# An opening list in another order, with statistics, inverse root and weight scale in smaller pieces and fewer dummy matmuls

## The chip, the core and the metric

The kernel runs on one core of a Trainium2 chip. The metric is the device time in microseconds (us) of one execution. The core has five engines that run side by side, each through its own instructions in order: TensorE (PE, matrix products), VectorE (DVE), ScalarE (ACT), GpSimd (POOL), and SyncE (SP), which here issues the DMA transfers. They wait for one another by semaphores. PE multiplies into PSUM banks, and what it has written there is read by DVE and ACT.

## What is computed

x has 2048 rows of 448 numbers. It is normalized row by row, goes through a filter in the frequency domain, and through an MLP with a gate; the results and x are added.

```python
def reference(A_x, A_w_r, A_w_i, B_x, B_W_gate, B_W_up, B_W_down):
    x = A_x
    xn = (x - mean) / sqrt(var + 1e-5)               # over the 448 columns
    A = irfft2(rfft2(xn) * (w_r + 1j * w_i))         # over rows and columns
    gate = xn @ W_gate                               # 448 x 1792
    up = xn @ W_up
    h = gate * (gate > 0) * up
    return x + A + h @ W_down                        # 1792 x 448
```

## The kernel before, in words

The rows are cut into 16 tiles of 128 (named by n2), and these into 4 chunks of 4 tiles; chunk q holds the tiles q, q+4, q+8 and q+12. The chunks come in the order 0, 2, 1, 3. The 1792 columns of W_gate and W_up are cut into 14 slabs f of 128, with g = 0 for gate and g = 1 for up. The slabs form groups of 5, 5 and 4; each group's part of h @ W_down is accumulated in PSUM for a chunk (dn, L923), with x or the sum so far as its start (dn_seed, L916, on ACT).

Products have nearly the precision of float32: each operand is split in two float16 parts, hi and lo, and three products are added (hi by hi, lo by hi, hi by lo). For weights, ACT writes hi (w_hi, L801) and DVE lo (w_lo, L805), after a common power of two has been found from the sum of the squares (w_sq, L189 on ACT; w_sum, L192 on POOL; w_scale, L195 and L199 on DVE). For a tile of rows the statistics (ln_stats, L255 and L258), the root (ln_sd, L266, ACT), the inverse root with one Newton step (ln_rstd, L271 to L276, DVE) give the normalized rows (ln_xn, L295); hi is made on ACT (L302, L304), lo on DVE (L332), and small rearranging copies on POOL (L311, L312, L333).

A matmul needs these tiles transposed, with the 448 columns on the partitions. The transposed tile of a chunk is named T; T_62 is that of the first chunk, T_63 that of the second. For the first chunk PE transposes against an identity matrix (L351), and the result is copied out of PSUM by DVE (vev, L359) or ACT (aev, L357); one block of 128 by 128 comes by a DMA transpose (d9, L345). From the second chunk on, the whole tile is transposed by DMA (dm, L341). A slab and chunk need 20 matmuls of 512 columns for each of gate and up (L852, gu; the first slab does them in halves of 256 columns), of which one step with only 64 partitions is shared by two slabs (L859). ACT then takes the positive part of the gate (L887), DVE multiplies it by up (L891), ACT writes its hi (L895) and DVE its lo (L899).

While all this runs, the Fourier part (L368 to L500 and L604 to L760) goes on beside it as background work, between the matmuls of the MLP.

Loads are issued by SP in order: x for statistics (load_xr, lx, L223, tiles y), x for the final sum (load_x, ly, L217, tiles xy), weight slabs (lw, L231, wst), W_down slabs (lwd, L241, wdst), Fourier constants (L245, fm), the identity (lid) and another constant, fd (lfd, both L1197).

**What sets the order.** The opening, up to the first group of 5 slabs of chunk 0, is written out by hand in OPENING (L29 to L41). Each word is a piece of work. In a block in which nothing is rescheduled (L1247 to L1257) the pieces are issued one after the other, so the list sets the order on every engine at once, DMA queue included. A piece is named by its step and its tile or slab: st0 is the statistics of tile 0, whiW0g1 the hi part of slab 0's up weights, tpA4 and tpB4 the first three and the other five transposes of tile 4, hh, lh and hl the three products of the first slab, gu2g1 all of slab 2's up, lo6 the lo part of tile 6, dm6 its DMA transpose. After the opening, a planner that counts the cost of each unit of PE work spreads the background work over the units; it starts from where the opening ended.

Dummy matmuls into spare PSUM banks (keep_warm, L1195, on a zeroed tile bw) stand at the beginning (warm, NWARM of them) and at three places in the opening (kw1, kw6, kw3).

## Time and profile before

| | |
| --- | --- |
| time, median of 3 runs | 443.38 us (443.28 to 443.58) |
| the profiled execution | 443.39 us |
| its span, first to last instruction | 441.6 us |
| mean granted TensorE clock | 0.999 |
| DMA, read from and written to HBM | 24.25 and 3.67 MB |

The span is what the engines' rows cover; 1.8 us of the time lie around it. In the rows below, a time is that from the start of the span, and of an engine's groups the count follows an x. "MATMUL gu<-T,wt" reads: the bank gu is written from T and wt. A bracket gives the idle time of the engine before the row, and which engine's tile ended it. SPq is SP's queue of transfers: its row says how long it took to issue, not how long the data took. A wait of an engine that waits for several things is put down to the one that came last.

### The profile page before, as it was taken

The numbers are of one execution on the slowest core, as the hardware profiler recorded it, in microseconds if no ns is written. First come the engines' busy times: TensorE is split into PE (matmuls) and PEld (weight loads), VectorE is DVE, ScalarE is ACT, GpSimd is POOL, SyncE is SP. The second block draws the span as 40 slices with busy tenths as digits, with TensorE's granted clock in tenths as the row PEclk, the third lists the DMA queues.
The fourth block names the chain that finished last, engine by engine and source line by source line (L and its number), as shares of the span: only waits on it lengthen the run. The fifth ranks groups of instructions, "written<-read, shape, count | busy, mean of one in ns | idle before, by whom it ended". The sixth has DMA issues, their size and how long they took to land.

```text
span 441.6 us, 8132 instructions
## 1 busy us (share of the span) xinstructions
PE 432.8 (98%) x3009; PEld 210.2 (48%) x3009; DVE 375.9 (85%) x922; ACT 254.3 (58%) x515; POOL 39.8 (9%) x84
## 2 busy tenths in 40 slices
...
GB/s 253 291 95 250 372 303 104 2 28 82 3 0 2 143 220 119 161 92 65 108 1 85 42 1 1 2 85 1 78 21 56 74 73 12 72 75 8 105 22 83
DMA packets 38360, 39.66 MB, mean 90 GB/s; under 512 B 18592, under 2 KB 33216, under 8 KB 38320
## 3 DMA queue, kind: packets, MB, share of 16 engines
...
q14 instruction: 17, 0.14, 0.1%
HBM read 24.25 MB, written 3.67 MB: 63 GB/s over the span
## 4 chain that ended last, share of the span: by engine, by line
PE 77%; DVE 13%; DMA 5%; SPq 2%; issue 1%; ACT 1%; POOL 0%; DVEq 0%; ACTq 0%
PE gu L852 44%; PE dn L923 23%; DMA sw<-wst 3%; PE gu L859 3%; PE fx L450 2%; DVE vt L715 1%; PE fx L417 1%; DVE g L891 1%; PE fx L723 1%; DMA y<-in_xr 1%; PE dn L955 1%; DVE h L899 1%; DMA xy<-in_x 1%; PE gu L955 1%; DVE wst L604 1%
## 5 line engine op out<-in xcount | busy, mean ns | idle before, releaser
L852 PE MATMUL gu<-T,wt 128*128 128x512 f16 (+1 forms) x1140 | 255.8, 376 | 1.6 <-DVE g L891 1.1
L852 PEld LDWEIGHTS <-wt 128*128 128x128 f16 x1140 | 108.7, 98 | 132.3 <-issue 10.7
L923 PE MATMUL dn<-wdt,h 128*128 128x448 f16 x624 | 127.6, 353 | 0.0
L923 PEld LDWEIGHTS <-h 128*128 128x128 f16 x624 | 60.2, 98 | 57.0
L895 ACT ACTIVATE h<-g 128x512 f16<-128x512 f32 x56 | 34.9, 626 | 65.1 <-DVE g L891 64.9
L887 ACT ACTIVATE g<-gu 128x512 f32<-128x512 f32 x56 | 33.0, 590 | 39.0 <-PE gu L859 23.5
L891 DVE SCALAR_TENSOR_TENSOR g<-gu,g 128x512 f32<-128x512 f32 x56 | 38.4, 686 | 18.6 <-ACT g L887 18.4
L899 DVE TENSOR_TENSOR h<-g,h 128x512 f16<-128x512 f32 x56 | 38.3, 685 | 6.0 <-ACT h L895 6.0
L927 ACT ACTIVATE xy<-dn,dsc 128x448 f32<-128x448 f32 x44 | 27.6, 630 | 25.1 <-PE dn L923 25.0
L192 POOL PARTITION_ALL_REDUCE wm<-wm x15 | 16.0, 1072 | 155.8 <-ACT junk L189 155.8
L916 ACT ACTIVATE dn<-xy,dinv 128x448 f32<-128x448 f32 x44 | 27.6, 632 | 0.5
L805 DVE SCALAR_TENSOR_TENSOR wt<-wst,wsc,wt 128x512 f16<-128x512 f32 x28 | 20.6, 748 | 1.0 <-ACT wt L801 1.0
L801 ACT ACTIVATE wt<-wst,wsc 128x512 f16<-128x512 f32 x28 | 19.2, 713 | 1.8 <-DVE wsc L199 1.8
L189 ACT ACTIVATE junk<-wst 128x512 bf16<-128x512 f32 x28 | 17.4, 621 | 0.9 <-DMA wst<-in_wgu 0.6
L859 PE MATMUL gu<-T,wt 64*128 64x512 f16 x112 | 17.0, 381 | 0.1
L732 DVE SCALAR_TENSOR_TENSOR wf<-fx,wf 128x512 f16<-128x512 f32 x16 | 10.9, 686 | 4.9 <-ACT wf L729 4.9
L255 DVE BATCH_NORM_STATS2 bst<-y 128x6 f32<-128x448 f32 x16 | 9.6, 613 | 5.8 <-DMA y<-in_xr 5.8
L440 ACT ACTIVATE Xh<-eo 128x464 f16<-128x464 f32 x16 | 8.9, 596 | 8.7 <-DVE eo L391 8.7
L710 ACT ACTIVATE vt<-wst,fsc 128x928 f16<-128x928 f32 x8 | 8.8, 1097 | 8.4 <-DVE wst L391 6.0
L470 DVE TENSOR_TENSOR y<-y,y 128x464 f32<-128x464 f32 x21 | 13.4, 638 | 0.2
L471 DVE TENSOR_TENSOR y<-y,y 128x464 f32<-128x464 f32 x21 | 13.4, 636 | 0.0
L723 PEld LDWEIGHTS <-vt 128*128 128x128 f16 x192 | 11.4, 98 | 2.0 <-issue 0.4
...
## 6 DMA issues: line engine op xcount, KB each, us to landing
...
```

Of the source, the lines that this page charges most:

```text
L189: A.activation(mt([128, 512], BF16, "junk")[:, 0:src.shape[-1]], src, AF.Square, scale=SQ, accum_out=acc)
L801: A.activation(w[:, 0:4, :], wst[f, g], AF.Copy, scale=wsc[f, g])
L805: V.scalar_tensor_tensor(w[:, 4:8, :], st, sc, w[:, 0:4, :], op0=OP.mult, op1=OP.subtract)
L852: last["P"] = P.matmul(hps[f, q][:, g, cs], wt[f, g][:, a, :], Tq[q][:, b, cs], start=(start and i == 0), stop=(stop and i == len(seq) - 1 ...
L859: m = P.matmul(hps[f, q][:, g, 0:512], wt[f, g][rows, 7, :], Tq[q][rows, b, :], start=start, stop=not start).ins
L887: last["A"] = A.activation(g1s[f, q], hps[f, q][:, 0, :], AF.Relu, scale=2.0 ** -22).ins
L891: last["V"] = V.scalar_tensor_tensor(g1, hps[f, q][:, 1, :], 2.0 ** -22, g1, op0=OP.mult, op1=OP.mult).ins
L895: A.activation(ht[f, q][:, 0, :], g1s[f, q], AF.Copy)
L899: V.tensor_tensor(h[:, 1, :], g1s.pop((f, q)), h[:, 0, :], op=OP.subtract)
L916: A.activation(dps[n2][:, 0:D], xy[n2], AF.Copy, scale=dinv[:, g:g + 1])
L923: last["P"] = P.matmul(dps[n2][:, 0:D], ht[f, q][:, a, js], wdt[f][:, b, :], start=False, stop=(f == fs[-1] and a == 1), skip_group_check= ...
L927: last["A"] = A.activation(xy[n2], dps[n2][:, 0:D], AF.Copy, scale=dsc[:, g:g + 1]).ins
```

## The change

1. NWARM goes from 19 to 14, and the three groups of dummies from 6, 3 and 1 to 5, 3 and 1, at other places.
2. OPENING is another order of nearly the same pieces. ln_stats becomes bn and ag, ln_rstd five pieces (ra to rm), w_scale wex and wsc, so that others may stand between them. Two evictions of the first tiles move from DVE to ACT (vevA0 and vevA4 become aevA0 and aevA4), one from ACT to DVE (aevB8 becomes vevB8).
3. Of the loads of x, ly0 and ly12 go from ahead of the DMA transposes to the end of the list, ly4 and ly8 stand ahead of them still. The DMA transposes of the ninth block (d9) come earlier in SP's queue, between weight loads, and lfd goes between two DMA transposes of the second chunk.
4. The tile bst gets 4 buffers for 2, and the hand list may begin a slab's bank with gate or up.

```diff
-NWARM = 19
+NWARM = 14
...
-lx0 lx4 lw lid lw lx8 lx12 lw lw lw lw lx2 lx10 lx6 lx14 lwd0 lwd1 lwd2 lwd3 lwd4 warm st0 st4 sqA rsA hi4
+lx0 lx4 bn0 bn4 ag0 ag4 sqA warm raA rbA rcA lw lid lx8 lx12 wsqW0g0 lw parW0g0 rdA rmA hi0 xn0 xn4 wexW0g0 lw cp0 lo0
...
-    def ln_stats(q, j):
-        n2 = q + 4 * j
-        st = ft([128, 6], F32, "bst", 2)
-        V.bn_stats(st, xr_t[n2])
+    def ln_bn(q, j):
+        bst[q, j] = ft([128, 6], F32, "bst", 4)
+        V.bn_stats(bst[q, j], xr_t[q + 4 * j])
+
+    def ln_ag(q, j):
         if j == 0:
             mv[q] = ft([128, 4, 2], F32, "mv", 2)
-        V.bn_aggr(mv[q][:, j, :], st)
+        V.bn_aggr(mv[q][:, j, :], bst.pop((q, j)))
...
-    def ln_rstd(q, js=(0, 1, 2, 3), bias=False):
+    def ln_r(step, q, js=(0, 1, 2, 3)):
...
+        if step == "a":
+            V.reciprocal(r0, sd)
+        elif step == "b":
...
+    def w_exp(f, gs=(0, 1)):
+        half_exponent(eg[:, f, gs[0]:gs[-1] + 1], state["wm", f][:, 1, gs[0]:gs[-1] + 1])
+
+    def w_pow(f, gs=(0, 1)):
         sc = mt([128, 2], F32, "wsc", 6)
-        e = eg[:, f, gs[0]:gs[-1] + 1]
-        half_exponent(e, state["wm", f][:, 1, gs[0]:gs[-1] + 1])
-        shift_exponent(sc[:, 0:len(gs)], e, -1, 188)
+        shift_exponent(sc[:, 0:len(gs)], eg[:, f, gs[0]:gs[-1] + 1], -1, 188)
...
-              **{f"kw{n}": (lambda n=n: keep_warm(n)) for n in (1, 3, 6)},
+              **{f"kw{n}": (lambda n=n: keep_warm(n)) for n in (1, 3, 5,)},
```

How the order moves is seen at three places. In the new order, lines of the program stand some 1 to 22 higher: L223 is L224, L266 is L274, L302 is L319, L357 is L374, L189 is L190, L801 is L823, L341 is L358, L891 is L913, L899 is L921, L443 is L460, L498 is L515, L859 is L881, and L1195 is L1217.

**ScalarE in the opening**, from the first root on. First the order before (tt_101 to tt_104 are the tiles of normalized rows, wt the weights' hi parts, junk,wm the sums of squares, fx the PSUM bank that PE transposes into):

```order
L266 ACTIVATE rs<-mv,eps 128x2
L302 ACTIVATE tt_101<-y_67,rs 128x448
L189 ACTIVATE junk,wm<-wst 128x512
L302 ACTIVATE tt_102<-y_66,rs 128x448
...
L801 ACTIVATE wt<-wst,wsc 128x512
...
L302 ACTIVATE tt_103<-y_68,rs 128x448
...
L302 ACTIVATE tt_104<-y_69,rs 128x448
...
L357 ACTIVATE T_62<-fx 128x3x128 x2
L357 ACTIVATE T_62<-fx 128x5x128 x2
```

And now:

```order
L190 ACTIVATE junk,wm<-wst 128x512
L319 ACTIVATE tt_101<-y_66,rs 128x448
L319 ACTIVATE tt_102<-y_67,rs 128x448
L374 ACTIVATE T_62<-fx 128x3x128
L823 ACTIVATE wt<-wst,wsc 128x512
L374 ACTIVATE T_62<-fx 128x3x128
L190 ACTIVATE junk,wm<-wst 128x512
L274 ACTIVATE rs<-mv,eps 128x2
L190 ACTIVATE junk,wm<-wst 128x512 x2
L319 ACTIVATE tt_103<-y_69,rs 128x448
L319 ACTIVATE tt_104<-y_68,rs 128x448
L374 ACTIVATE T_62<-fx 128x3x128 x2
```

A sum of squares has moved ahead of the first tile, and two evictions that DVE made before now stand among the first six rows. One eviction of five transposes follows behind, where before there were two.

**SP's queue from the second chunk's DMA transposes on**, before:

```order
L341 DMA_TRANSPOSE T_63<-tt_101 128x9x128
L341 DMA_TRANSPOSE T_63<-tt_103 128x9x128
L341 DMA_TRANSPOSE T_63<-tt_102 128x9x128
L341 DMA_TRANSPOSE T_63<-tt_104 128x9x128
L245 DMA fm<-in_c_fm 128x1024
L231 DMA wst<-in_wgu 128x512 x2
...
L217 DMA xy<-in_x 128x448 x4
L223 DMA y_82<-in_xr 128x448
L223 DMA y_83<-in_xr 128x448
```

And now (y_82 is the first tile of the third chunk, chunk 1):

```order
L358 DMA_TRANSPOSE T_63<-tt_103 128x9x128
L1219 DMA fd_t<-in_c_fd 128x464
L358 DMA_TRANSPOSE T_63<-tt_101 128x9x128
L358 DMA_TRANSPOSE T_63<-tt_104 128x9x128
L358 DMA_TRANSPOSE T_63<-tt_102 128x9x128
L246 DMA fm<-in_c_fm 128x1024
L232 DMA wst<-in_wgu 128x512 x2
L218 DMA xy<-in_x 128x448 x3
...
L218 DMA xy<-in_x 128x448 x2
...
L218 DMA xy<-in_x 128x448
L224 DMA y_82<-in_xr 128x448
L224 DMA y_83<-in_xr 128x448
```

The transposes come in another order of tiles, with fd's load behind the first. Between them and y_82 stood 10 loads (two fm, four wst, four xy); now there are 12, since six xy stand there. The rows left out repeat fm and wst.

**VectorE behind the statistics of chunk 1**, before:

```order
L330 SCALAR_TENSOR_TENSOR tt_104<-y_66,rs,tt_104 128x448
L330 SCALAR_TENSOR_TENSOR tt_104<-y_66,rs,tt_104 128x64
L891 SCALAR_TENSOR_TENSOR g_1038<-gu,g_1038 128x512
L498 TENSOR_TENSOR y_76<-y_77,fx 128x464
L499 TENSOR_TENSOR y_79<-y_77,fx 128x464
L443 TENSOR_TENSOR Xh<-eo,Xh 128x464 x2
L899 TENSOR_TENSOR h<-g_1038,h 128x512
```

And now:

```order
L347 SCALAR_TENSOR_TENSOR tt_104<-y_66,rs,tt_104 128x448
L347 SCALAR_TENSOR_TENSOR tt_104<-y_66,rs,tt_104 128x64
L515 TENSOR_TENSOR y_74<-y_73,fx 128x464
L516 TENSOR_TENSOR y_80<-y_73,fx 128x464
L460 TENSOR_TENSOR Xh<-eo,Xh 128x464 x2
L913 SCALAR_TENSOR_TENSOR g_1032<-gu,g_1032 128x512
L921 TENSOR_TENSOR h<-g_1032,h 128x512
```

The product of gate and up (L891, now L913), which frees two banks of PE, has moved behind four operations of the Fourier part. An L899 that stood behind the first statistics of chunk 1 now stands ahead of them.

More of the change, by code (lines that the diff above doesn't have):

```diff
@@ L279, in ln_rstd @@
         for i, j in enumerate(js):
-            rst[q, j] = r[:, i:i + 1], nm[:, i:i + 1], m[:, i, 0:1]
+            rst[q, j, "r"] = r[:, i:i + 1], nm[:, i:i + 1], m[:, i, 0:1]
+    def ln_rstd(q, js=(0, 1, 2, 3)):
+        for step in "abcdm":
+            ln_r(step, q, js)
     xn, tt, xn_b = {}, {}, {}
@@ L293, in ln_xn @@
         xn[n2] = xn_b[n2].rearrange("p g c k -> p (g c k)")[:, 0:D]
[L294 removed]
+        r, _, mean = rst[n2 % 4, n2 // 4, "r"]
         V.tensor_scalar(xn[n2], xr_t[n2], mean, r, op0=OP.subtract, op1=OP.mult)
@@ L1221, in gu_slab, with gu_part @@
     def gu_slab(f, g):
-        if f % 2 == 0 and g == 0:
+        if f % 2 == 0 and (f, q) not in hps:
             gu_open(f, q)
         gu_full(f, q, (g,), slice(0, 512), f % 2 == 0, f % 2 == 1)
+    def gu_part(f, q, *a):
+        if (f, q) not in hps:
+            gu_open(f, q)
+        gu_full(f, q, *a)
     for f in groups[0]:
```

61 lines of the change are left out of this document (35 added, 26 removed).

## The prediction

> **What bounds the kernel now.** I read the shares of the engines first, then the chain that ended last, then the list of what the TensorE (PE) waited for.
>
> ```profile
> PE 432.8 (98%) x3009; PEld 210.2 (48%) x3009; DVE 375.9 (85%) x922; ACT 254.3 (58%) x515; POOL 39.8 (9%) x84
> PE 77%; DVE 13%; DMA 5%; SPq 2%; issue 1%; ACT 1%; POOL 0%; DVEq 0%; ACTq 0%
> PE fx L351 <- DVE tt L332: 1.7, 2, 1.2
> PE dn L1195 <- POOL bw L1252: 1.5, 1, 1.5
> PE gu L852 <- DVE g L891: 1.1, 1, 1.1
> PE fx L351 <- ACT wt L801: 0.5, 1, 0.5
> ```
>
> PE is busy 98% of the span of 441.6 us, and its waits (total, times, longest) are few. Of those shown all but the 1.1 us for L891, late in the kernel, lie in the opening. So time can be won only in two ways: PE is given less to do, or its waits in the opening shrink. The opening matters beyond its waits, because it also holds dummy matmuls (L1195), which count as busy but compute nothing.
>
> ```profile
> 1.49 7.03 PE L1195 MATMUL dn<-bw 128*128 128x512 f16 x19 [1.49 <-POOL bw L1252]
> 10.62 1.46 PE L1195 MATMUL dn<-bw 128*128 128x512 f16 x6
> 12.80 0.81 PE L1195 MATMUL dn<-bw 128*128 128x512 f16 x3
> 15.54 0.44 PE L351 MATMUL fx<-id_t,tt 128*128 128x128 f16 x5
> 16.88 3.00 PE L852 MATMUL gu<-T,wt 128*128 128x256 f16 x26
> 19.90 0.60 PE L859 MATMUL gu<-T,wt 64*128 64x512 f16 x4
> 34.87 4.27 PE L852 MATMUL gu<-T,wt 128*128 128x512 f16 x19 [0.45 <-DVE wt L805]
> 39.07 0.61 PE L859 MATMUL gu<-T,wt 64*128 64x512 f16 x4
> 43.94 0.35 PE L923 MATMUL dn<-wdt,h 128*128 128x448 f16 x1
> 68.61 1.67 PE L852 MATMUL gu<-T,wt 128*128 128x512 f16 x7
> ...
> 1.40:7.00 5.60, 5.51 (x13) 1.00 0.80 241
> 7.00:8.30 1.30, 1.30 (x7) 1.00 0.96 351
> ```
>
> The first ten rows are PE's timeline (start, length, count, and in brackets the idle time before), the last two the windows of PE. Six dummies take 1.46 us and three 0.81 us, so one more costs (1.46 - 0.81) / 3 = 0.217 us at full pace. Up to 7.00 us 13 of them began, 5.60 / 13 = 0.43 us apart; behind it they are 0.22 apart (1.30 us for six intervals), although both rows give the granted clock as 1.00.
>
> **The change, part by part. Dummy matmuls.** 19 become 14, and groups of 6, 3 and 1 become 5, 3 and 1: six fewer. Fourteen at 0.43 from 1.49 end near 7.5, so the five that go are full-pace ones: 6 x 0.217 = 1.30 us less PE work. That becomes time only if what they covered is ready earlier. The next terms ask that.
>
> **First slab, set by ACT.** The changed order of ScalarE (ACT), shown with the change, has two more evictions of three transposes and one fewer of five.
>
> ```profile
> 6.29 0.76 ACT L302 ACTIVATE tt<-y,rs 128x448 f16<-128x448 f32 x1 [1.02 <-DVE rs L276]
> 8.22 0.62 ACT L189 ACTIVATE junk<-wst 128x512 bf16<-128x512 f32 x1
> 8.74 0.19 ACT L189 ACTIVATION_READ_ACCUMULATOR junk<-wst 128x1 f32 x1
> 9.80 0.29 ACT L266 ACTIVATE rs<-mv,eps 128x2 f32<-128x2 f32 x1 [0.87 <-DVE mv L258]
> 13.29 0.72 ACT L801 ACTIVATE wt<-wst,wsc 128x512 f16<-128x512 f32 x1 [0.61 <-DVE wsc L199]
> 15.30 0.49 ACT L357 ACTIVATE T<-fx 128x384 f16<-128x384 f16 x1
> ```
>
> The first normalized tile can end at 6.29 + 0.76 = 7.05 as before: the reordered statistics chain has the same steps, and the sum of squares now ahead of it in the queue fills ACT's 1.02 us of idle time. From there to the end of the last needed eviction ACT runs three more tiles (3 x 0.76), four evictions (4 x 0.49), two high halves of weights (2 x 0.72), three sums of squares (3 x 0.81) and one root (0.29): 8.40 us, hence 15.5 us. Behind it PE has 23 matmuls of 256 columns (3.00 / 26 = 0.115 each) and five transposes (at most 0.44): 3.0 us, so the first slab's last piece (L859) starts near 18.5, where it starts at 19.90 now. That is 1.4 us, about the 1.30 of the dummies; waits stay as long in sum as now. ACT idling would shrink it, and bounds are 0.5 and 2.5 us, but the next term caps the gain anyway. The split of statistics and inverse root adds no operation; VectorE (DVE) has three tensor copies where it had four. I cost the split at nothing: the small steps stand between larger ones of a queue that is full anyway, and if that cover went, each of them would cost PE some 0.2 us.
>
> **Transposes of the second chunk, the first cap.** PE reaches the second chunk's tile (T_63) at 39.07 with no wait. Freed of 1.4 us, and of the 0.45 us at 34.87 (that slab's VectorE half, L805, now stands three rows earlier in its order), PE would be there at 37.2. Then it meets SyncE's (SP's) transposes.
>
> ```profile
> 28.78 0.76 DVE L332 TENSOR_TENSOR tt<-y,tt 128x448 f16<-128x448 f32 x2
> 29.53 0.23 POOL L333 COPY tt<-tt 128x56 f16<-128x56 f16 x1 [7.91 <-DVE tt L332]
> 30.21 0.64 POOL L312 COPY tt<-tt 128x64 f16<-128x64 f16 x1
> 30.87 2.81 SPq L341 DMA_TRANSPOSE T<-tt  x2
> 34.29 2.74 SPq L341 DMA_TRANSPOSE T<-tt  x2
> 13.88 0.33 SPq L1197 DMA_DIRECT2D fd_t<-in_c_fd  x1
> ```
>
> Four transposes are queued at 1.4 us each, with 34.29 - 33.68 = 0.61 us of waiting for the third tile in between, and end at 37.03; PE's use at 39.07 bounds the landing at 2.04 us behind. In the new order the first of them is released by its own low half and its POOL copy. That low half has 71 VectorE operations ahead of it in either order, with one copy less and one small operation more now; before, the first transpose also stood behind two other tiles' POOL copies (29.53 to 30.85), now only behind its own. It can begin between 28.9 (PE's lead fully passed on, short copies) and 30.9 (nothing passed on); I take 29.7, PE's lead of 1.4 less what VectorE's full queue keeps. The load of fd now sits between the first and second transposes: +0.33. So 29.7 + 4 x 1.4 + 0.33 = 35.6 at the queue, and 37.7 landed. **PE gains 39.07 - 37.7 = 1.4 us here**, between 0.2 and 2.
>
> **Loads behind the transposes, the second cap.** Three things wait in SP's queue for the transposes: constants, weights, and rows of x for the residual (xy) and for chunk 1 (y). Two xy loads that stood ahead of the transposes now stand between them and y.
>
> ```profile
> 40.08 2.01 SPq L217 DMA_DIRECT2D xy<-in_x  x4
> 42.14 3.23 SPq L223 DMA_DIRECT2D y<-in_xr  x4
> 41.38 1.18 ACT L916 ACTIVATE dn<-xy,dinv 128x448 f32<-128x448 f32 x2
> 48.48 1.23 DVE L255 BATCH_NORM_STATS2 bst<-y 128x6 f32<-128x448 f32 x2 [2.21 <-DMA y<-in_xr]
> 52.49 0.64 DVE L368 TENSOR_TENSOR bw<-eo 128x464 f32<-128x464 f32 x1 [0.57 <-ACT eo L422]
> 57.87 1.19 DVE L443 TENSOR_TENSOR Xh<-eo,Xh 128x464 f16<-128x464 f32 x2 [0.60 <-ACT Xh L440]
> 66.63 0.68 DVE L891 SCALAR_TENSOR_TENSOR g<-gu,g 128x512 f32<-128x512 f32 x1
> 67.23 0.62 DVE L498 TENSOR_TENSOR y<-y,fx 128x464 f32<-128x464 f32 x1
> ...
> 40.00:50.00 10.00, 10.00 (x50) 4.59 (x47) 6.99 (x13) 5.43 (x11) 0.00 (x0) 1.00 1.00 369
> ```
>
> VectorE stands still 2.21 us for y until 48.48, the eleventh load behind the transposes; the last row (windows) shows all DMA engines busy then, 369 GB/s. In the new order y is the thirteenth: 448 KB more, 1.24 us at that rate. Counted from transposes that end 1.4 earlier, y lands at 48.48 - 1.4 + 1.24 = 48.3: as late by the clock as now, while PE is 1.4 ahead. VectorE then has, up to its next L891 (66.63, 18.15 us behind), three rows moved ahead of it and one taken out: two of L498's kind (0.62) and two of L443's (1.19 for both), less one of 0.66 (L899, estimated as L891): +1.8. Its two idle times of 0.57 and 0.60 go, since PE and ACT are ahead: -1.17. So that L891 ends at 48.3 + 18.15 + 1.8 - 1.17 + 0.68 = 67.8. PE wants its bank at 68.61 - 1.4 = 67.2. **Loss 0.55 us**, with bounds of 0 (no slow start of the loads) and 1.3 (the whole stretch from transposes to y grows in proportion, 11.4 us x 448 / 2656 KB = 1.9 in place of 1.24, which gives 1.2).
>
> The residual rows of the first accumulator now come fourth behind the transposes. By the same two rules they land between 40.0 and 42.6; ACT's seed (0.59 of the row at 41.38) has to follow before PE's first L923, at 43.94 - 1.4 = 42.5. Cost 0 to 0.7, **I take 0.15**.
>
> **Sum.** Against the profiled execution's own 443.39 us (span 441.6 and 1.8 around it; the median is 443.38): 443.39 - 1.4 + 0.55 + 0.15 = 442.7 us. Behind 70 us I expect a plain shift: PE's order reads alike in the last third, and its late wait of 1.1 us follows PE's own evictions.
>
> [...] The two windows above bear on the warm-up: pace 0.43, then 0.22, changing 5.5 us after the first dummy. [...]
>
> **The rivals.**
>
> (a) *No late stall.* y comes before 47.7, since the slow start of the queue is not repeated. For it: at 369 GB/s 2,656 KB need 7.4 us, and the stretch took 11.4. Then only the first cap holds: 443.39 - 1.4 = 442.0, or 441.7 with a faster start of the transposes. Chance 0.27.
>
> (b) *The change moves nothing measurable:* T_63 starts as late as now on VectorE's full queue, and fd's load in between eats the 0.3 left. The third tile's wait of 0.61 stays. Time 443.1 to 443.6. Chance 0.12.
>
> (c) *Slower: residual and y loads hold PE.* At the stretch's mean pace 13 loads take 13.3 us and y lands at 48.9; with a slow start that is 1 us longer it lands at 50, and L891 ends at 69.4 against 67.2: 2.2 lost, 1.4 won, and 0.3 lost on the seed: 444.5. It decides from a landing of 49.0 on, where gain and loss meet. VectorE is nearly full afterwards, so it cannot catch up:
>
> ```profile
> 80.00:100.00 20.00, 20.00 (x190) 9.90 (x189) 19.76 (x54) 15.03 (x29) 4.38 (x12) 1.00 0.12 23
> ```
>
> (third pair of numbers: VectorE 19.76 of 20 us). Against it: PE waited for nothing there before. Chance 0.10.
>
> (d) *Warm-up too short.* PE's pace is 0.43 until about 14 us. Then 9 dummies and about 17 matmuls of 256 columns each double (9 x 0.217 + 17 x 0.115 = 3.9), less 2.1 us of waits that they fill: +1.8, for 444.5. If it ends by 10.5, few matmuls are touched and the cost is about 0.2. Chance of the dear one 0.05.
>
> **How the numbers follow.** The forecast, 442.7 with its own range of 442.2 to 443.3, has 0.46; the rivals 0.27, 0.12, 0.10 and 0.05. A measurement of this kernel can tell about 0.2%, 0.9 us, from no change, so faster means below 442.5 and slower above 444.3. Faster: (a) and a quarter of the forecast, 0.39. Same: the rest of the forecast, (b) and some of (c), 0.47. Slower: 0.14. The range, 441.7 to 444.0, leaves out the dear ends of (c) and (d) and the low end of (a), some 0.2.
>
> **What would show it.** In the changed profile: L859's first group near 18.5; transposes into T_63 starting near 29.7 with fd's load between; PE's first T_63 matmul near 37.7 with some 0.5 us of wait ahead of it; VectorE's statistics on y at 48 to 48.6; a PE wait for L913 near 67. The prediction is wrong if statistics on y start before 47.5 (then (a)) or behind 49.0 (then (c)), if T_63 is used behind 38.7 (then (b)), if the dummies keep 0.43 behind 8.3 us (then (d)), or if PE shows waits between 70 and 300 us.

## The result, and the profile after

The changed kernel takes 447.92 us, median of 6 runs (446.83 to 449.6), against 443.48 (443.14 to 444.24) in as many of the kernel before: a ratio of 1.0101, with a 95% interval of 1.0074 to 1.0128. It is slower by some 4.5 us, and the forecast of 442.7 (441.7 to 444.0) was wrong, in sign and in size. The profiled execution took 449.6, its span is 447.8.

The engines' shares, the longest of PE's waits, and rows of PE's timeline in the changed kernel, which answer to the rows of before:

```profile
PE 435.4 (97%) x3003; PEld 210.3 (47%) x3003; DVE 374.8 (84%) x921; ACT 254.3 (57%) x516; POOL 43.4 (10%) x84
PE gu L881 <- DVE wt L827: 3.8, 1, 3.8
...
19.43 0.61 PE L881 MATMUL gu<-T,wt 64*128 64x512 f16 x4
32.62 1.03 PE L881 MATMUL gu<-T,wt 64*128 64x512 f16 x4 [3.85 <-DVE wt L827]
33.59 11.04 PE L874 MATMUL gu<-T,wt 128*128 128x512 f16 x40
44.56 0.60 PE L881 MATMUL gu<-T,wt 64*128 64x512 f16 x4
```

PE does six dummies less, yet it is busy for 2.6 us more (435.4 against 432.8). The first slab's last piece starts at 19.43, where it started at 19.90: 0.5 us won. Then stands a wait that the kernel before does not have, 3.85 us, ahead of the second pair of slabs. The 40 matmuls behind it take 11.04 us, where 40 took 8.81 before the wait. The second chunk's tile is reached at 44.56, where it was 39.07: 5.5 us behind. Of the 6.2 us by which the span is longer (447.8 against 441.6), these 5.5 stand there already.

Who holds PE? The wait is followed back through VectorE and ScalarE to SP's queue. These are the timelines of ScalarE, VectorE, SP (for SP: how long it took to issue) and POOL:

```profile
22.97 1.32 ACT L823 ACTIVATE wt<-wst,wsc 128x512 f16<-128x512 f32 x2
28.75 0.58 ACT L190 ACTIVATE junk<-wdst 128x448 bf16<-128x448 f32 x1 [4.46 <-DMA wdst<-in_wd]
30.60 0.57 ACT L909 ACTIVATE g<-gu 128x512 f32<-128x512 f32 x1
...
31.21 0.69 DVE L913 SCALAR_TENSOR_TENSOR g<-gu,g 128x512 f32<-128x512 f32 x1 [4.36 <-ACT g L909]
31.82 0.74 DVE L827 SCALAR_TENSOR_TENSOR wt<-wst,wsc,wt 128x512 f16<-128x512 f32 x1
...
12.28 5.25 SPq L362 DMA_TRANSPOSE T<-tt  x2
17.64 0.52 SPq L232 DMA_DIRECT2D wst<-in_wgu  x1
18.69 2.91 SPq L362 DMA_TRANSPOSE T<-tt  x1
23.21 1.38 SPq L242 DMA_DIRECT2D wdst<-in_wd  x3
...
16.18 0.39 POOL L350 COPY tt<-tt 128x56 f16<-128x56 f16 x2
```

Read it from PE backwards. PE waits until 32.62 for a low half of weights (L827), which VectorE begins at 31.82. VectorE is in order, and ahead of this stands a product of gate and up (L913, at 31.21) that waits 4.36 us for ScalarE's gate (L909, at 30.60). ScalarE is in order too: ahead of the gate stands the sum of squares of W_down's slab 0 (L190 on wdst), and for that load ScalarE stands still for 4.46 us, until 28.75. The load is the second of the three issued from 23.21 on, so it was issued near 23.7, and 5.1 us passed until ScalarE could use it. SP came to it so late because two small DMA transposes, put ahead of it, held SP from 12.28 to 17.53 (the second had to wait for its tile, whose last copies on POOL are the row at 16.18), and a third took 2.91 us to issue. In the kernel before, the five loads of W_down stood ahead of the transposes and of the weight loads that follow; this is its row:

```profile
9.46 3.01 SPq L241 DMA_DIRECT2D wdst<-in_wd  x5
```

Last, the clock. Windows of PE in the changed kernel (stretch, its length, busy time, then granted clock, DMA share and rate):

```profile
28.00:30.00 2.00, 0.77 (x4) 1.00 0.14 44
30.00:32.00 2.00, 0.00 (x0) 0.83 0.01 4
36.00:38.00 2.00, 2.00 (x6) 0.50 0.66 126
38.00:40.00 2.00, 2.00 (x11) 0.96 1.02 201
```

The granted clock falls to 0.50 inside the wait and comes back at about 38.2 (0.96 over the window from 38 to 40). PE starts 6 matmuls in the window at 0.50 and 11 in that at 0.96. That is why the 40 matmuls take 11.04 us, and not 8.81.

### The profile page after: what moved, and what is told of

Same layout as the page of the kernel before. It is cut to its first block, busy times and chain, and to the rows that moved or that the text cites. A ratio compares the mean times of both kernels' runs of the same rounds, so it can differ in the third digit from the quotient of the medians.

```text
span 447.8 us, 8119 instructions
## 1 busy us (share of the span) xinstructions
PE 435.4 (97%) x3003; PEld 210.3 (47%) x3003; DVE 374.8 (84%) x921; ACT 254.3 (57%) x516; POOL 43.4 (10%) x84
## 3 DMA queue, kind: packets, MB, share of 16 engines
q1 hardware_dynamic: 38320, 39.14, 28.8%
## 4 chain that ended last, share of the span: by engine, by line
PE 68%; DVE 13%; DMA 10%; SPq 4%; ACT 2%; issue 1%; POOL 1%; DVEq 0%; ACTq 0%
PE gu L874 39%; PE dn L945 20%; DMA sw<-wst 3%; PE gu L881 3%; DMA wst<-in_wgu 2%; PE fx L467 2%; DVE vt L732 1%; DMA fm<-in_c_fm 1%; PE fx L740 1%; DMA wdst<-in_wd 1%; DVE h L921 1%; DMA xy<-in_x 1%; PE dn L977 1%; DVE g L913 1%; DMA y<-in_xr 1%
## 5 line engine op out<-in xcount | busy, mean ns | idle before, releaser
L874 PE MATMUL gu<-T,wt 128*128 128x512 f16 (+1 forms) x1140 | 258.4, 378 | 2.6 <-DVE g L913 1.3
L913 DVE SCALAR_TENSOR_TENSOR g<-gu,g 128x512 f32<-128x512 f32 x56 | 38.3, 685 | 24.3 <-ACT g L909 24.1
L909 ACT ACTIVATE g<-gu 128x512 f32<-128x512 f32 x56 | 33.0, 589 | 43.6 <-PE gu L881 24.9
L921 DVE TENSOR_TENSOR h<-g,h 128x512 f16<-128x512 f32 x56 | 38.3, 685 | 9.3 <-ACT h L917 9.3
L827 DVE SCALAR_TENSOR_TENSOR wt<-wst,wsc,wt 128x512 f16<-128x512 f32 x28 | 20.5, 744 | 4.3 <-ACT wt L823 4.3
L881 PE MATMUL gu<-T,wt 64*128 64x512 f16 x112 | 17.4, 390 | 4.0 <-DVE wt L827 3.8
L823 ACT ACTIVATE wt<-wst,wsc 128x512 f16<-128x512 f32 x28 | 19.1, 713 | 0.1
L190 ACT ACTIVATE junk<-wst 128x512 bf16<-128x512 f32 x28 | 17.5, 624 | 2.7 <-DMA wst<-in_wgu 2.4
L328 POOL COPY tt<-tt 128x56 f16<-128x56 f16 x16 | 8.1, 508 | 54.2 <-ACT tt L337 51.3
```

What stands on the lines that cost most here:

```text
L190: A.activation(mt([128, 512], BF16, "junk")[:, 0:src.shape[-1]], src, AF.Square, scale=SQ, accum_out=acc)
L823: A.activation(w[:, 0:4, :], wst[f, g], AF.Copy, scale=wsc[f, g])
L827: V.scalar_tensor_tensor(w[:, 4:8, :], st, sc, w[:, 0:4, :], op0=OP.mult, op1=OP.subtract)
L874: last["P"] = P.matmul(hps[f, q][:, g, cs], wt[f, g][:, a, :], Tq[q][:, b, cs], start=(start and i == 0), stop=(stop and i == len(seq) - 1 ...
L881: m = P.matmul(hps[f, q][:, g, 0:512], wt[f, g][rows, 7, :], Tq[q][rows, b, :], start=start, stop=not start).ins
L909: last["A"] = A.activation(g1s[f, q], hps[f, q][:, 0, :], AF.Relu, scale=2.0 ** -22).ins
```

## The experiments

Theory T: the late load of W_down holds ScalarE's queue, and through it VectorE and PE. Rival C: the shortened warm-up lets the clock fall. Rival S: transposes among the loads slow all of them. For the smaller terms of the prediction further runs follow. Times are medians, the ratios against runs of the kernel before that were made with them on the same chip.

### Two loads exchanged

```diff
-bn10 wscW2 lh10 hl01 bn2 ag2 ag14 ag6 hl11 lwd4 wsqW3g1 parW3 lh11 hp0 gu1g1 re0 wexW3 whiW2g1 d90 ag10 wscW3 lwd2 lw
-whiW2g0 gu1g0 ly8 tm0 sqC raC whiW3g0 wloW2g1 lwd1 whiW3g1 lwd0 gu2g1 wdq0 rbC wsqW4g0 wloW3g0 rcC gh0 re1 lwd3
+bn10 wscW2 lh10 hl01 bn2 ag2 ag14 ag6 hl11 lwd0 wsqW3g1 parW3 lh11 hp0 gu1g1 re0 wexW3 whiW2g1 d90 ag10 wscW3 lwd2 lw
+whiW2g0 gu1g0 ly8 tm0 sqC raC whiW3g0 wloW2g1 lwd1 whiW3g1 lwd4 gu2g1 wdq0 rbC wsqW4g0 wloW3g0 rcC gh0 re1 lwd3
```

> The changed kernel with two words of the opening list exchanged: the load of W_down's slab 0 now stands where that of slab 4 stood, four loads earlier, and slab 4's in its place. Every instruction stays where it is on every engine. Theory T (the late load): in the changed kernel ScalarE stands still 4.46 us at 24.29 for W_down's slab 0, which lands at 28.67; behind it in ScalarE's queue is the gate of slab 1, behind that VectorE's low half of slab 3, and for this PE waits 3.85 us at 28.77. Now slab 0 should land near 23.6, ScalarE should not wait there, PE's 3.85 us should fall to under 1, the clock should stay at 1.00, and the time should be 442.5 to 444. [...] Rival S (the transposes among the loads slow every load): the wait only moves to slab 4's low-priority sum of squares, and 446 or more stays.

444.39 us, ratio 1.0019 (1.0009 to 1.0028), some 0.4 us above the expected range. 3.5 of the 4.5 us are gone with the exchange of two loads, and not one instruction of a compute engine has moved. PE's rows, then VectorE's row for y and SP's rows for the large transposes:

```profile
28.58 0.61 PE L881 MATMUL gu<-T,wt 64*128 64x512 f16 x4
39.09 0.61 PE L881 MATMUL gu<-T,wt 64*128 64x512 f16 x4 [0.77 <-DMA T<-tt]
69.56 4.48 PE L874 MATMUL gu<-T,wt 128*128 128x512 f16 x20 [0.61 <-DVE g L913]
...
49.92 1.24 DVE L257 BATCH_NORM_STATS2 bst<-y 128x6 f32<-128x448 f32 x2 [2.72 <-DMA y<-in_xr]
...
30.38 1.34 SPq L358 DMA_TRANSPOSE T<-tt  x1
32.45 4.46 SPq L358 DMA_TRANSPOSE T<-tt  x3
```

The wait at 28.8 is gone, and the clock stays at 0.999 or 1.000 in all ten runs. What is left are the waits that the prediction spoke of: the large transposes (0.77 at 39.09) and VectorE behind y (0.61 at 69.56). Rival C, for which the exchange of two loads changes nothing, and rival S fall as the cause of the large loss.

### The small transposes behind the loads

```diff
-wloW0g1 hh11 vevB8 aevB12 whiW1g0 wloW1g0 whiW1g1 d94 d912 wsqW2g1 wloW1g1 wsqW2g0 parW2 bn6 wsqW3g0 bn14 lw wexW2
-bn10 wscW2 lh10 hl01 bn2 ag2 ag14 ag6 hl11 lwd4 wsqW3g1 parW3 lh11 hp0 gu1g1 re0 wexW3 whiW2g1 d90 ag10 wscW3 lwd2 lw
-whiW2g0 gu1g0 ly8 tm0 sqC raC whiW3g0 wloW2g1 lwd1 whiW3g1 lwd0 gu2g1 wdq0 rbC wsqW4g0 wloW3g0 rcC gh0 re1 lwd3
-wloW2g0 rdC xn14 hi14 xn6 wsqW4g1 hi6 parW4 xn10 hi10 tm1 wloW3g1 cp10 cp14 xn2 gu2g0 wexW4 d98 wdq4 wdq2 lo10 dm10
+wloW0g1 hh11 vevB8 aevB12 whiW1g0 wloW1g0 whiW1g1 wsqW2g1 wloW1g1 wsqW2g0 parW2 bn6 wsqW3g0 bn14 lw wexW2
+bn10 wscW2 lh10 hl01 bn2 ag2 ag14 ag6 hl11 lwd4 wsqW3g1 parW3 lh11 hp0 gu1g1 re0 wexW3 whiW2g1 ag10 wscW3 lwd2 lw
+whiW2g0 gu1g0 ly8 tm0 sqC raC whiW3g0 wloW2g1 lwd1 whiW3g1 lwd0 gu2g1 wdq0 rbC wsqW4g0 wloW3g0 rcC gh0 re1 lwd3 d94 d90 d912 d98
+wloW2g0 rdC xn14 hi14 xn6 wsqW4g1 hi6 parW4 xn10 hi10 tm1 wloW3g1 cp10 cp14 xn2 gu2g0 wexW4 wdq4 wdq2 lo10 dm10
```

> The changed kernel with the four small DMA transposes (ninth block) put behind all W_down loads in SyncE's queue, as they stand in the kernel before; nothing else moves. Theory T, with the transposes as the cause that the loads are late: all five W_down loads land before 22 us, PE's wait of 3.85 us goes, 442.5 to 444. If the position of the W_down loads alone made them late, and the transposes among them cost nothing, W_down's slab 0 still lands behind 26 us and 446 or more stays. Rival C: no change, 447 to 450.

444.88 us, ratio 1.0033 (1.0020 to 1.0046). ScalarE's wait for the load shrinks from 4.46 to 0.74 us. Rows of SP and ScalarE:

```profile
9.86 6.17 SPq L232 DMA_DIRECT2D wst<-in_wgu  x3
17.97 1.38 SPq L242 DMA_DIRECT2D wdst<-in_wd  x3
24.68 0.58 ACT L190 ACTIVATE junk<-wdst 128x448 bf16<-128x448 f32 x1 [0.74 <-DMA wdst<-in_wd]
```

Slab 0's load, the second of the three, is issued near 18.45 here, 5.2 us earlier than in the changed kernel. So the transposes ahead of the loads cost these 5.2 us, and most of ScalarE's wait. They are not all of the lateness: in the kernel before, slab 0's load was issued at 9.46, and here SP stands until 15.7 in front of the third weight load, for a buffer that VectorE (L827, whose row there ends at 15.62) has to free. The expectation that all five loads land before 22 us was missed: ScalarE could use slab 0 only at 24.68, 6.2 us after its issue. The time came 0.9 us above the expected range; the large transposes started at 31.45 here, 1.1 us later than in the run before.

### Nineteen dummies at the beginning

```diff
-NWARM = 14
+NWARM = 19
```

> The changed kernel with 19 dummy matmuls at the beginning in place of 14; nothing else moves. Theory T: the wait of 3.85 us is set by a load and not by PE's pace, so it only shrinks by what PE arrives later (about 1 us), and the time stays at 446.8 to 449.6. Rival C (too short a warm-up): the clock stays at 1.00 and the time falls to 443 to 445.

447.94 us, ratio 1.0102 (1.0087 to 1.0117): as slow as the changed kernel, as T says and against rival C, which had 443 to 445. Rows of ScalarE and PE, and a window of PE:

```profile
26.97 0.58 ACT L190 ACTIVATE junk<-wdst 128x448 bf16<-128x448 f32 x1 [3.27 <-DMA wdst<-in_wd]
30.83 0.61 PE L881 MATMUL gu<-T,wt 64*128 64x512 f16 x4 [2.66 <-DVE wt L827]
...
32.00:34.00 2.00, 2.00 (x7) 0.56 0.00 0
```

ScalarE's 3.27 and PE's 2.66 differ by 0.61; in the changed kernel 4.46 and 3.85 differ by 0.61 too. The wait passes through one for one. It is shorter than in the changed kernel because slab 0 came 1.8 us earlier (26.97 against 28.75), and not because PE came later, as expected: PE stood from 28.17 on, where it was 28.77. The clock fell here too, near 32.2, 1.4 us behind the end of the wait.

### ScalarE's sum of squares moved, the loads left

```diff
-whiW2g0 gu1g0 ly8 tm0 sqC raC whiW3g0 wloW2g1 lwd1 whiW3g1 lwd0 gu2g1 wdq0 rbC wsqW4g0 wloW3g0 rcC gh0 re1 lwd3
-wloW2g0 rdC xn14 hi14 xn6 wsqW4g1 hi6 parW4 xn10 hi10 tm1 wloW3g1 cp10 cp14 xn2 gu2g0 wexW4 d98 wdq4 wdq2 lo10 dm10
+whiW2g0 gu1g0 ly8 tm0 sqC raC whiW3g0 wloW2g1 lwd1 whiW3g1 lwd0 gu2g1 rbC wsqW4g0 wloW3g0 rcC gh0 re1 lwd3
+wloW2g0 rdC xn14 hi14 xn6 wsqW4g1 hi6 parW4 xn10 hi10 tm1 wloW3g1 cp10 cp14 xn2 gu2g0 wexW4 d98 wdq0 wdq4 wdq2 lo10 dm10
```

> The changed kernel with its loads untouched, but the sum of squares of W_down's slab 0 moved back in ScalarE's own queue, behind the last tile of chunk 2, next to those of the slabs 4 and 2 (the order behind the opening changes by 68 of PE's rows with it). Theory T in its second half, that it is ScalarE's in-order queue that carries the late load to PE: ScalarE does not wait at 24.3, PE's wait at 28.8 is under 1 us, and the time is 443.5 to 445. If PE waited for a late weight load itself and not for the queue: 446.5 or more stays.

444.63 us, ratio 1.0022 (1.0013 to 1.0031). Slab 0's load is issued near 22.6, about as late as in the changed kernel (23.7 and, in its second profile below, 22.2), but PE does not wait at 28.6:

```profile
28.62 0.60 PE L881 MATMUL gu<-T,wt 64*128 64x512 f16 x4
```

The order behind the opening changed with this edit in some of PE's rows, but not ahead of this one. This shows the second half of T: the order of ScalarE's queue carried the load's delay to PE.

### The same in the kernel before

```diff
-lx0 lx4 lw lid lw lx8 lx12 lw lw lw lw lx2 lx10 lx6 lx14 lwd0 lwd1 lwd2 lwd3 lwd4 warm st0 st4 sqA rsA hi4
+lx0 lx4 lw lid lw lx8 lx12 lw lw lw lw lx2 lx10 lx6 lx14 warm st0 st4 sqA rsA hi4
...
-wloW0g1 lw lfd hh01 hh11 whiW1g0 st2 lh01 lh10 whiW1g1 hl01 wloW1g0 lw hl11 wsqW2g0 wloW1g1 lw ly0 ly4 ly8
+wloW0g1 lw lfd hh01 hh11 whiW1g0 st2 lh01 lh10 whiW1g1 hl01 wloW1g0 lw hl11 wsqW2g0 wloW1g1 lw lwd0 lwd1 lwd2 lwd3 lwd4 ly0 ly4 ly8
```

> The kernel before, with its five W_down loads moved in SyncE's queue from ahead of the last four weight loads to behind them, just ahead of the x rows and the small transposes; every instruction of the other engines stays in its place. Theory T (a late W_down load holds ScalarE's queue and through it PE): slab 0 of W_down then lands near 23, ScalarE, which wants it at 21.15, stands still for about 2 us there, PE gets a wait of 0.5 to 2 us near 28 that the kernel before does not have, and the time is 444 to 445.5. If the loss in the changed kernel came from something else of the new order, this stays at 443.0 to 443.8.

445.29 us, ratio 1.0041 (1.0028 to 1.0055). ScalarE's and PE's rows:

```profile
23.66 0.58 ACT L189 ACTIVATE junk<-wdst 128x448 bf16<-128x448 f32 x1 [2.58 <-DMA wdst<-in_wd]
26.65 4.48 PE L852 MATMUL gu<-T,wt 128*128 128x512 f16 x20 [1.77 <-DVE g L891]
```

Late loads of W_down alone, with no transposes ahead of them, make the kernel before slower by the same road: 2.58 us on ScalarE, 1.77 us on PE (here through VectorE's product L891).

### The wait filled with dummies

```diff
-cp6 wscW4 whiW4g0 hi2 wdq3 lfd hp2 gu3g1 gu3g0 lo6 re2 lo14 gl0 cp2 dm14 lo2 wdq1 tm2 wloW4g0 gh2 wdp whiW4g1 wdsc dm2
+cp6 wscW4 whiW4g0 hi2 wdq3 lfd kw17 hp2 gu3g1 gu3g0 lo6 re2 lo14 gl0 cp2 dm14 lo2 wdq1 tm2 wloW4g0 gh2 wdp whiW4g1 wdsc dm2
...
-              **{f"kw{n}": (lambda n=n: keep_warm(n)) for n in (1, 3, 5,)},
+              **{f"kw{n}": (lambda n=n: keep_warm(n)) for n in (1, 3, 5, 17)},
```

> The changed kernel with 17 dummy matmuls (17 x 0.216 = 3.7 us) just ahead of the PE instruction that waits 3.85 us, so that PE is busy through nearly all of the wait. It measures what the clock's drop behind the wait costs by itself (11.04 us for 40 matmuls in place of 8.81 in the profiled execution). If the drop follows from PE standing idle: no run shows a clock below 0.999, and the time is 446.5 to 447.2 in all of them, the level of the changed kernel's runs with clock 1.00. If it has another cause: some runs still come out near 449 with a clock of 0.992 to 0.996.

448.65 us (448.05 to 452.04), ratio 1.0117 (1.0100 to 1.0134). Four of five runs had a clock of 0.999 or 1.000, but at 448.05 to 449.33 they were slower than expected. In the fifth, the profiled one (0.996), it fell in a later wait. Its rows of PE and ScalarE, with 17 dummies up to the end of the first wait:

```profile
50.28 4.68 PE L945 MATMUL dn<-wdt,h 128*128 128x448 f16 x15 [2.20 <-ACT dn L938]
...
49.59 1.19 ACT L938 ACTIVATE dn<-xy,dinv 128x448 f32<-128x448 f32 x2 [5.25 <-DMA xy<-in_x]
```

So the filling kept the clock up at the first wait (1.00 in all windows from 28 to 42), but the times that were expected of that did not come. In the profiled execution PE lost 2.20 us to the residual rows, for which ScalarE stood still 5.25 us. The order behind the opening also differed in some of PE's rows, so what the clock costs is not measured by this run.

### The changed kernel once more

> The changed kernel once more, unedited, for the clock alone: of its six runs three had a mean granted clock of 0.992 to 0.996 and took 448.8 to 449.6, three had 0.999 to 1.000 and took 446.8 to 447.1. If a fall of the clock behind PE's wait of 3.85 us costs time by itself, the runs divide in the same two groups, some 2 us apart. If the division was chance (in the run with 19 dummies at the beginning it was not seen: 447.7 to 448.1 with the low clock, 448.4 with the full one), clock and time do not go together.

446.90 us, 445.51 to 449.87 in six runs, ratio 1.0093 (1.0068 to 1.0119). The one run with a low clock, 0.992, took 449.87, but one with 0.999 took 448.36, so the groups are not clean. Its profiled execution (446.42) shows why they spread; rows of SP, ScalarE and PE:

```profile
18.11 1.11 SPq L362 DMA_TRANSPOSE T<-tt  x1
25.86 0.58 ACT L190 ACTIVATE junk<-wdst 128x448 bf16<-128x448 f32 x1 [2.15 <-DMA wdst<-in_wd]
29.72 0.61 PE L881 MATMUL gu<-T,wt 64*128 64x512 f16 x4 [1.53 <-DVE wt L827]
41.19 0.61 PE L881 MATMUL gu<-T,wt 64*128 64x512 f16 x4 [0.77 <-DMA T<-tt]
```

Here the third small transpose took 1.11 us to issue, not 2.91, ScalarE waited 2.15 us, not 4.46, and PE 1.53, not 3.85; the clock stayed at 1.00 in all windows from 28 to 42. The same program has a wait of 1.5 to 3.9 us. Of the 2.9 us by which slab 0 came earlier here (25.86 against 28.75), 1.5 are its earlier issue (near 22.2 against 23.7), and 1.4 a shorter way from issue to use (3.7 us against 5.1). The transpose is thus only part of it: in the run with 19 dummies at the beginning it took 1.18 us, and the load still took 5.1 us. What sets that time is not shown. From the end of PE's wait to the second chunk's tile it took 41.19 - 29.72 = 11.47 us with the full clock, and 44.56 - 32.62 = 11.94 with the fallen one. The fall of the clock thus cost some 0.47 us in that execution, not the 2.2 us by which the matmuls were longer, since with the full clock PE waits 0.77 us for the transposes instead, and 0.89 at two places in between. In the run with 19 dummies at the beginning the clock fell as well, and the same way took 42.30 - 30.83 = 11.47 us, no longer than with the full clock.

### Six dummies less, in the kernel before

```diff
-NWARM = 19
+NWARM = 14
...
-xn4 xn0 wsqW0g0 cp4 st8 hi0 parW0g0 st12 wsqW0g1 cp0 tpA0 lo0 tpA4 kw1 wscW0g0 sqB tpB0 kw6 parW0g1 wsqW1g0
+xn4 xn0 wsqW0g0 cp4 st8 hi0 parW0g0 st12 wsqW0g1 cp0 tpA0 lo0 tpA4 kw1 wscW0g0 sqB tpB0 kw5 parW0g1 wsqW1g0
...
-              **{f"kw{n}": (lambda n=n: keep_warm(n)) for n in (1, 3, 6)},
+              **{f"kw{n}": (lambda n=n: keep_warm(n)) for n in (1, 3, 5)},
```

> The kernel before with the changed kernel's number of dummy matmuls (14 at the beginning, the group of six cut to five), nothing else moved. Theory T: the opening is set by the engines that feed PE, so six dummies less are worth little: PE starts the first slab at most 0.3 us earlier, and the time is 443.0 to 443.6, the same. If the dummies set PE's pace through the opening, as the prediction's first term has it: 442.1 to 442.4. If the warm-up becomes too short for the clock: 444 or more, with the granted clock or the dummies' spacing showing it.

443.92 us, ratio 1.0010 (0.9999 to 1.0020): no gain, as T expected, though 0.3 us above its range, and a hint of rival C. Five of eleven runs had a clock of 0.991 to 0.996 and took 443.9 to 444.5; the six with 0.999 or 1.000 took 443.0 to 443.9. The profile is of the first kind, with its PE rows and windows:

```profile
10.61 0.64 PE L351 MATMUL fx<-id_t,tt 128*128 128x128 f16 x5 [1.48 <-DVE tt L332]
11.04 2.34 PE L1195 MATMUL dn<-bw 128*128 128x512 f16 x5
20.27 0.61 PE L859 MATMUL gu<-T,wt 64*128 64x512 f16 x4
...
10.00:11.00 1.00, 0.39 (x5) 0.87 1.05 402
11.00:12.00 1.00, 1.00 (x6) 0.50 1.05 399
```

From 7.6 to 10.6 PE has little to do, the clock falls to 0.50, five dummies take 2.34 us, and the first slab's last piece starts at 20.27, where it was 19.90. So in the order before, the dummies taken away helped to keep the clock up across this gap: of the 16 runs of the kernel before made beside these, two had such a clock (0.995).

### The order of the loads put back

fd's load behind the large transposes, with the exchanged W_down loads:

```diff
-cp6 wscW4 whiW4g0 hi2 wdq3 lfd hp2 gu3g1 gu3g0 lo6 re2 lo14 gl0 cp2 dm14 lo2 wdq1 tm2 wloW4g0 gh2 wdp whiW4g1 wdsc dm2
-re3 wloW4g1 wdh3 dm6 gh1 gu4g0 tm3 wdh1 wdh4 wdl3 wdh0 gh3 wdl1 gu4g1 hp4 wdh2 gl2 gl1 re4 wdl0 wdl2 tm4 wdl4 gh4 gl3
+cp6 wscW4 whiW4g0 hi2 wdq3 hp2 gu3g1 gu3g0 lo6 re2 lo14 gl0 cp2 dm14 lo2 wdq1 tm2 wloW4g0 gh2 wdp whiW4g1 wdsc dm2
+re3 wloW4g1 wdh3 dm6 lfd gh1 gu4g0 tm3 wdh1 wdh4 wdl3 wdh0 gh3 wdl1 gu4g1 hp4 wdh2 gl2 gl1 re4 wdl0 wdl2 tm4 wdl4 gh4 gl3
```

> The changed kernel with the exchange of the two W_down loads, and with fd's load put behind the four large transposes in place of between the first and the second. In the exchange run PE waited 0.77 us at 39.09 for these transposes, and fd stood in their queue for 0.73 us (31.72 to 32.45). If that load's place is what the wait is made of, the transposes land near 38.1, the wait falls below 0.2, and the time is 443.6 to 444.0. If not, because each transpose waits for its tile anyway, 444.2 to 444.6 as in the exchange run.

446.05 us, ratio 1.0056 (1.0043 to 1.0070): slower than with fd in between, against the expectation. PE had no wait for the transposes any more, but it waited 0.6 us for the residual rows, and y came later, so that VectorE stood still for 3.90 us until 50.87. The order of a few rows behind the opening changed with this edit, so it does not measure fd's place by itself.

The two loads of x put back ahead of the transposes, in addition:

```diff
-whiW2g0 gu1g0 ly8 tm0 sqC raC whiW3g0 wloW2g1 lwd1 whiW3g1 lwd4 gu2g1 wdq0 rbC wsqW4g0 wloW3g0 rcC gh0 re1 lwd3
+whiW2g0 gu1g0 ly8 tm0 sqC raC whiW3g0 wloW2g1 lwd1 whiW3g1 lwd4 gu2g1 wdq0 rbC wsqW4g0 wloW3g0 rcC gh0 re1 lwd3 ly0 ly12
...
-ly0 ly12 gl4
+gl4
```

> As the one before, and the two loads of x for the residual that the change had put behind the large transposes are back ahead of them, behind the W_down loads. Prediction's second cap: statistics of chunk 1 wait for the y load behind 12 others, and PE loses 0.61 us at 69.56 for it. With two loads (1.2 us) less in front, the statistics should start 1.2 us earlier against PE, the wait at 69.5 should go, ScalarE's 2.29 us of waiting for the first xy too, and the time should be 442.9 to 443.5, no slower than the kernel before. If the wait at 69.5 comes from the new order of VectorE alone, it stays at 0.4 or more and the time at 443.6 to 444.

444.75 us, ratio 1.0029 (1.0017 to 1.0040): a miss as well, for the wait at 69.4 stayed at 0.60. VectorE's row shows that y still came late, though fewer loads stand ahead of it; why is not shown:

```profile
49.01 1.21 DVE L257 BATCH_NORM_STATS2 bst<-y 128x6 f32<-128x448 f32 x2 [4.16 <-DMA y<-in_xr]
```

Then the whole of SP's order as in the kernel before, under the changed order of the other engines:

```diff
-hl00 ly4 xn8 lw lx6 tpA12 hl10 kw1 hi8 cp8 tpA8 lo12 tpB12 aevA12 lx10 aevA8 lh01 wexW1 lx2 lw lw lo8 tpB8 hh01 wscW1
-wloW0g1 hh11 vevB8 aevB12 whiW1g0 wloW1g0 whiW1g1 d94 d912 wsqW2g1 wloW1g1 wsqW2g0 parW2 bn6 wsqW3g0 bn14 lw wexW2
-bn10 wscW2 lh10 hl01 bn2 ag2 ag14 ag6 hl11 lwd4 wsqW3g1 parW3 lh11 hp0 gu1g1 re0 wexW3 whiW2g1 d90 ag10 wscW3 lwd2 lw
-whiW2g0 gu1g0 ly8 tm0 sqC raC whiW3g0 wloW2g1 lwd1 whiW3g1 lwd0 gu2g1 wdq0 rbC wsqW4g0 wloW3g0 rcC gh0 re1 lwd3
-wloW2g0 rdC xn14 hi14 xn6 wsqW4g1 hi6 parW4 xn10 hi10 tm1 wloW3g1 cp10 cp14 xn2 gu2g0 wexW4 d98 wdq4 wdq2 lo10 dm10
-cp6 wscW4 whiW4g0 hi2 wdq3 lfd hp2 gu3g1 gu3g0 lo6 re2 lo14 gl0 cp2 dm14 lo2 wdq1 tm2 wloW4g0 gh2 wdp whiW4g1 wdsc dm2
+hl00 xn8 lw lx6 tpA12 hl10 kw1 hi8 cp8 tpA8 lo12 tpB12 aevA12 lx10 aevA8 lh01 wexW1 lx2 lw lw lo8 tpB8 hh01 wscW1
+wloW0g1 hh11 vevB8 aevB12 whiW1g0 wloW1g0 whiW1g1 lwd0 lwd1 lwd2 lwd3 lwd4 lfd wsqW2g1 wloW1g1 wsqW2g0 parW2 bn6 wsqW3g0 bn14 lw wexW2
+bn10 wscW2 lh10 hl01 bn2 ag2 ag14 ag6 hl11 wsqW3g1 parW3 lh11 hp0 gu1g1 re0 wexW3 whiW2g1 ag10 wscW3 lw
+whiW2g0 gu1g0 ly0 ly4 ly8 ly12 d90 d94 d98 d912 tm0 sqC raC whiW3g0 wloW2g1 whiW3g1 gu2g1 wdq0 rbC wsqW4g0 wloW3g0 rcC gh0 re1
+wloW2g0 rdC xn14 hi14 xn6 wsqW4g1 hi6 parW4 xn10 hi10 tm1 wloW3g1 cp10 cp14 xn2 gu2g0 wexW4 wdq4 wdq2 lo10 dm10
+cp6 wscW4 whiW4g0 hi2 wdq3 hp2 gu3g1 gu3g0 lo6 re2 lo14 gl0 cp2 dm14 lo2 wdq1 tm2 wloW4g0 gh2 wdp whiW4g1 wdsc dm2
...
-ly0 ly12 gl4
+gl4
```

> The changed kernel with SyncE's loads and transposes back in the order of the kernel before (W_down loads, then fd, then the last weights, then four xy, then the small transposes, then the large ones); PE's order is that of the changed kernel throughout, and VectorE's and ScalarE's but for 6 and 2 rows. Theory T: the loss of the change lies in the order of the loads. Then ScalarE does not stand still at 24, PE has no wait at 28.8, the large transposes land before 38.6, and the time is 442.8 to 444.0. If the pieces' order on the compute engines costs by itself, 444.5 or more is left.

443.55 us, ratio 1.0000 (0.9991 to 1.0009). The loss is gone altogether, with all of PE's rows in the changed order, and VectorE's and ScalarE's but for a few: **the change's loss lies in its order of the loads**. Rows of PE and of VectorE:

```profile
19.08 0.61 PE L881 MATMUL gu<-T,wt 64*128 64x512 f16 x4
28.36 0.61 PE L881 MATMUL gu<-T,wt 64*128 64x512 f16 x4
38.42 0.61 PE L881 MATMUL gu<-T,wt 64*128 64x512 f16 x4 [0.33 <-DVE h L921]
364.25 4.48 PE L874 MATMUL gu<-T,wt 128*128 128x512 f16 x20 [1.08 <-DVE g L913]
...
47.69 1.83 DVE L257 BATCH_NORM_STATS2 bst<-y 128x6 f32<-128x448 f32 x3 [2.82 <-DMA y<-in_xr]
```

With the statistics of y at 47.69 the wait near 69 does not come up. PE is 0.65 us ahead at the second chunk (38.42 against 39.07) and keeps 0.2 of it at its late wait, which began its matmul at 364.44 in the kernel before:

```profile
364.44 4.48 PE L852 MATMUL gu<-T,wt 128*128 128x512 f16 x20 [1.11 <-DVE g L891]
```

And 29 dummies again in this version:

```diff
-NWARM = 14
+NWARM = 19
...
-tpA0 hi4 aevA0 wscW0g0 tpA4 whiW0g0 lw bn8 bn12 ag8 tpB0 kw3 aevA4 ag12 lw hh00 kw5 wsqW0g1 sqB wloW0g0 parW0g1 cp4
+tpA0 hi4 aevA0 wscW0g0 tpA4 whiW0g0 lw bn8 bn12 ag8 tpB0 kw3 aevA4 ag12 lw hh00 kw6 wsqW0g1 sqB wloW0g0 parW0g1 cp4
...
-              **{f"kw{n}": (lambda n=n: keep_warm(n)) for n in (1, 3, 5,)},
+              **{f"kw{n}": (lambda n=n: keep_warm(n)) for n in (1, 3, 6)},
```

> As the one before, with 29 dummies again (19 at the beginning, a group of six). The difference of the two is what six dummies less are worth in the new order. By the prediction's first term 1.3 us at the first slab; by the two runs so far (ScalarE's chain sets the first slab: 0.6 us gained at 19.3 in the exchange run) 0.3 to 0.7 us there, and at the end 0 to 0.5: 443.0 to 444.5.

443.53 us, ratio 1.0000 (0.9991 to 1.0008). PE's rows:

```profile
19.28 0.60 PE L881 MATMUL gu<-T,wt 64*128 64x512 f16 x4
38.69 0.61 PE L881 MATMUL gu<-T,wt 64*128 64x512 f16 x4
```

With six dummies less PE is 0.2 us ahead at the first slab, 0.27 at the second chunk, and nothing can be measured at the end. Even the 0.2 is less than what two executions of the unedited changed kernel differ by at the first slab (18.84 and 19.43), so it cannot be told from nothing.

## Why the prediction was wrong

**The step that failed** is in the paragraph on the transposes of the second chunk: "PE would be there at 37.2". It took PE to run from the first slab to the second chunk without a new wait, and the paragraph on loads named three things in SP's queue behind the large transposes, but none between the small ones. The W_down loads, which the change moved from ahead of the small transposes to among them, appear in no step, and the list of the change does not name them either, though the opening's order shows it. Moved loads have a first reader on some queue; here it is ScalarE's sum of squares, wanted at 24.3 (the end of the row at 22.97), and delivered at 28.75. That was 3.85 us in the profiled execution, and by the exchange run 3.5 us of the median.

**Dummies, 1.30 us less work: right as work, nearly nothing as time.** The prediction said so itself ("only if what they covered is ready earlier"), and then let ScalarE's ledger pass 1.4 us on. The runs with and without them differ by 0.2 us at the first slab, which is within the spread of one kernel.

**First slab at 18.5: 18.84 and 19.43 in two executions of the changed kernel.** The ledger of ScalarE left out its waiting. The sum of squares that was to fill idle time waits 1.17 us for its weights, until 6.30, so that the first normalized tile begins at 6.93 and not at 6.29. Later ScalarE waits 1.68 us for PE's transposes before the evictions, and PE waits 0.56 us for a copy on POOL, and 0.96 for the eviction; these rows are ScalarE's and PE's:

```profile
6.30 0.63 ACT L190 ACTIVATE junk<-wst 128x512 bf16<-128x512 f32 x1 [1.17 <-DMA wst<-in_wgu]
15.62 1.47 ACT L374 ACTIVATE T<-fx 128x384 f16<-128x384 f16 x3 [1.68 <-PE fx L368]
15.36 0.23 PE L368 MATMUL fx<-id_t,tt 128*128 128x128 f16 x1 [0.56 <-POOL tt L329]
16.55 0.49 PE L874 MATMUL gu<-T,wt 128*128 128x256 f16 x3 [0.96 <-ACT T L374]
```

The gain of 1.4 is 0.5 to 1.1.

**Large transposes from 29.7, PE at 37.7, gain 1.4:** in the runs of the changed order in which PE does not wait near 28.6 they began at 30.07 to 31.45. In the exchange run the whole gain is lost in three steps: they began at 30.38 (0.68 later than forecast), took 6.53 us in SP's queue against 5.93 (0.60 more), and PE could use them 2.18 us behind that against 2.04 (0.14 more), at 39.09. The 0.60 is a mis-sized term: 4 x 1.4 leaves out the 0.61 us that the row of before shows between the second and the third transpose, and that rival (b) let stay. In the new order such a gap stands behind the first one. fd's load is hardly to blame: with it the second transpose starts 2.07 us behind the first, and without it, in the run with SP's order of before, 1.95 us. There PE was at 38.42 (gain 0.65).

**The loss of 0.55 us near 67 to 69 behind y: right in mechanism, its size by luck.** With the late load out of the way it was 0.61 us at 69.56, and with y at 47.69 it was 0, as rival (a) had it. y came at 49.92 and not at 48.3, 1.6 us late, and PE wanted its bank at 68.95 and not at 67.2, 1.75 us late: two errors that cancelled. What was right by itself is VectorE's way from y to the end of the product, forecast as 19.5 us and 19.6 here.

**The residual rows, 0.15 us:** PE waited nothing for them in the exchange run, though ScalarE waited 2.29 us. The wait exists all the same: 0.6 us with fd behind the transposes, and 2.20 us in the profiled execution with the wait filled.

**Behind 70 us, a plain shift:** not quite. With SP's order of before, 0.65 us of lead became 0.2 by the late wait; the planner's order behind the opening is another one, and its pieces were not told apart.

**Rivals.** In the changed kernel PE used T_63 at 44.56 and VectorE's statistics on y began at 54.86, which are the signs of rivals (b) and (c), but both only follow PE's wait at 28.77. Rival (c) named loads that hold PE, but other ones, later. Rival (d) let the pace of 0.43 last until about 14 us, or until 10.5; both times were the author's suppositions. In the two profiles of the unedited changed kernel it did not last so long: the group of three dummies, at 9.02 and 8.26, took 0.81 us as before, and the group of five, at 10.07 and 9.48, 1.24 us. The clock did fall later, in a wait, and cost some 0.47 us net in one execution and, in the run with 19 dummies at the beginning, nothing; in the kernel before with 23 dummies it fell in the opening of the profiled execution, and five of eleven runs had a mean of 0.991 to 0.996.
